# Attention with mixed heads: output matmuls of 128 keys on the whole height of the TensorE array instead of 64-key halves, and a third PSUM bank for the first mix

## The chip, the cores and the metric

The kernel runs on one core of a Trainium2 chip. The metric is the device time of one execution in microseconds (us); lower is better. The core has five engines with instruction queues of their own: PE (TensorE, matmuls; the profile shows its weight loads apart, as PEld), DVE (VectorE), ACT (ScalarE), POOL (GpSimd) and SP (SyncE, which here only issues DMAs).

## The reference

Talking-heads attention over 4 batches, 12 heads, 448 positions and head dimension 64, then a two-layer network with an ELU between. All arrays are float32.

```python
scores = scale * np.matmul(q, k.transpose(0, 1, 3, 2))      # (4, 12, 448, 448)
scores = np.einsum('bhij,hg->bgij', scores, w_pre)           # first mix over the heads
scores = scores - np.max(scores, axis=-1, keepdims=True)
attn = np.exp(scores)
attn = attn / (np.sum(attn, axis=-1, keepdims=True) + 1e-09)
attn = np.einsum('bhij,hg->bgij', attn, w_post)              # second mix over the heads
out = np.matmul(attn, v)                                     # (4, 12, 448, 64)
...
h = x @ w_in                                                 # x: 1792 x 768, w_in: 768 x 2048
g = np.where(h > 0.0, h, np.exp(np.minimum(h, 0.0)) - 1.0)
return g @ w_out                                             # 2048 x 768
```

## The kernel before

**The attention** goes through 16 blocks (4 batches times 4 blocks of query rows). A block has 10, 12, 12 or 11 *tiles* of 10 rows, which makes 180 tiles. Two tiles make a *step* (the last step of an 11-tile block has one), so there are 92 steps, and the loop over `j` in `attention` writes the instructions of all engines in a fixed order. One round of the loop issues, in this order on PE:

- `scores` for step j+2, the first mix (tile `s`, L223): 4 matmuls of 448 columns, into one PSUM bank for each of the two tiles. Then DVE takes the row maximum (`nm`, L228) and ACT the exponential with its sum (`p`, L230), which frees the bank.
- `qk` for one pair of heads of a later block (L189): 4 matmuls of 448 columns. DVE and ACT copy them out (`st`, L199) and SP sends them by DMA into `raw`, the layout in which the first mix reads all heads of a row at once.
- `av` (L281), a part of attention times V for an earlier block, described below.
- `post` for step j, the second mix (tiles `mixed`, L256): small matmuls with `p` as weights and the scaled mixing matrix `wz` (POOL, L243) as the moving operand, then two ACT copies into `at` (L263).

Every one of these matmuls uses a 64 x 64 quarter of the PE array: a half of its rows (the 64 partitions on which the operands lie) and a half of its columns (the 64 partitions of the result). Four of them, one for each quarter, can be under way together. All operands are float32, for which one matmul of the program becomes two passes on PE, each a weight load (LDWEIGHTS) and a MATMUL row in the trace.

**Keys.** The 448 keys lie in `at` as NJ = 4 chunks of 128 partitions; the last chunk has 64 keys. In `post` each tile has 7 pieces of 64 keys. Before, six pieces go to the upper and the lower half of the first three chunks, and the seventh is split by heads: half of the heads are put on the upper 64 partitions of chunk 3, half on the lower 64 (the order `PLACE` of the heads makes each half contiguous). The parts of chunk 3 that nobody writes hold zeros.

**Outputs.** `av(n, u, part)` makes the outputs of two pairs of heads (w = 0, 1) of block n. Upper and lower 64 keys of a chunk are separate matmuls that sum into separate PSUM banks (`half`), since the two row halves of the array run at once. With the split chunk this is 7 rounds of 4 quarters, 28 matmuls of 100, 110 or 120 columns; 4 rounds are issued in one step and 3 in the next (`parts`). `keep_av` then copies the first bank to SBUF and adds the second one (DVE, L295 and L296). There are 48 such groups (16 blocks times 3).

**PSUM.** Eight banks during the attention: 2 for `s`, 2 for `mixed`, 2 for `qk`, 2 for `av`.

**The network** (`Moe`) follows: 128 x 128 matmuls `h` (L500) and `y` (L570). Its first matmuls are mixed into the last steps of the attention. Besides, the weights are decoded on DVE, ACT and POOL all along (`Weights`).

Of the kernel before, what the change touches and what calls it, by code (L numbers as in the profile page):

```python
# [17 lines left out]
B, H, S, D = 4, 12, 448, 64  # L18
DM, DFF = H * D, 2048
R = 10  # L20
RH = R * H
HR = R // 2
# [3 lines left out]
CJ = 128  # L26
# [5 lines left out]
EPS = 1e-9  # L32
PLACE = [g for w in range(2) for g in range(H) if g // 2 % 2 == w]

# [85 lines left out]
def attention(ctx, tc, qd, kd, vd, wpre, wpost, xd, dec, moe):  # L120
# [93 lines left out]


    def scores(n, ts):
        z = small.tile([128, 2], F32, tag="z", name="z")
        got = []
        ps = [bank(ps_s, "s", 2) for _ in ts]
        for w in range(2):  # L220
# [26 lines left out]
    def post(pairs):  # L247
        for i, (p, wz) in enumerate(pairs):
            for c in range(NJ):
                for h in range(2):  # L250
                    half = slice(h * 64, (h + 1) * 64)
                    j, n = (c * CJ + h * 64, slice(0, RH // 2)) if c < NJ - 1 else (
                        c * CJ, slice(h * RH // 4, (h + 1) * RH // 4))
                    for w in range(2):
                        part = slice(w * 64, (w + 1) * 64)
                        nc.tensor.matmul(  # L256
                            mixed[w][half, i, c, n], p[part, j:j + 64], wz[part, n], start=True, stop=True)

# [8 lines left out]

    def av(n, u, part):
        m = count[n] * R
        if part.start == 0:  # L270
            xo[n, u] = [bank(*spare) for half in range(2)]
        ps = xo[n, u]
        full = [(w, c) for w in range(2) for c in range(NJ - 1)]
        todo = list(zip([(0, NJ - 1)] + full, full[:NJ - 1] + [(1, NJ - 1)] + full[NJ - 1:]))
        for todo in todo[part]:
            for half, (w, c) in enumerate(todo):
                part = slice(half * 64, (half + 1) * 64)
                hp = 2 * u + w
                for hh in range(2):
                    g = PLACE.index(2 * hp + hh)  # L280
                    nc.tensor.matmul(  # L281
                        ps[half][hh * 64:(hh + 1) * 64, w * m:(w + 1) * m].rearrange("p (t r) -> p t r", r=HR),
                        vs[blocks[n][0], hp][part, c, hh * 64:(hh + 1) * 64],
                        ats[n][part, c, :count[n], :, g * HR:(g + 1) * HR].rearrange("p t w r -> p (t w) r"),
                        start=c == (NJ - 1 if half == w else 0), stop=c == NJ - 2,
                    )

    def keep_av(n, u):
        b, i = blocks[n]
        m = count[n] * R  # L290
        if u == 0:
            x = xp.tile([128, NP * 120], F32, tag="x", name="x")
            xs[n] = x[:, :NP * m].rearrange("p (c m) -> p c m", c=NP)
        lo, hi = (ps[:, :2 * m].rearrange("p (w m) -> p w m", w=2) for ps in xo.pop((n, u)))
        nc.vector.tensor_copy(xs[n][:, 2 * u:2 * u + 2], lo)  # L295
        nc.vector.tensor_add(xs[n][:, 2 * u:2 * u + 2], xs[n][:, 2 * u:2 * u + 2], hi)  # L296

# [7 lines left out]
    for ps in mixed:  # L305
        nc.vector.memset(ps[:, :, NJ - 1], 0.0)
    load_q(0, nc.sync)
# [18 lines left out]
    work, qks, avs = {}, {}, {}  # L326
    spare = ps_qk, "av", 2

# [10 lines left out]
    V_AT = -4, -3, 3, 4, 5, 6  # L339
    parts = slice(0, 4), slice(4, 7)  # L340
    ends = [N - 11, N - 9, N - 7, N - 5, N - 3, N - 1, N, N + 1, N + 2]
# [11 lines left out]
    for n in range(NBL):  # L353
        b, i = blocks[n]
        for u in range(3):
            if n < NBL - 3:
                for part, j in zip(parts, OUT_AT[i][2 * u:2 * u + 2]):
                    avs.setdefault(b * ROUND + j, []).append((n, u, part))
            else:
                avs.setdefault(ends.pop(0), []).append((n, u, slice(0, 7)))  # L360
    for b in range(B):
# [5 lines left out]
    for j in range(-LOOK, N + 3):  # L367
        if j == N - 10:
            op_ctx.close()
            dec.early = None  # L370
            moe.begin()
            spare = moe.ps[0], "ps", 2, 2
        if j == N:
            spare = ps_s, "s", 2
        if j in FIRST and j >= N:
# [8 lines left out]
        ready = [(n, keep_qk(n, [(hp, qk(n, hp))])) for n, hp in todo[:1]]  # L384
        for n, u, part in avs.get(j, ()):
            av(n, u, part)
            if part.stop == 7:
                keep_av(n, u)
                if u == 2 and j < N:
                    plan(j + 1, lambda n=n: store_x(n))  # L390
                elif u == 2:
                    store_x(n)
# [187 lines left out]
def lay_out(q, k, v, w_pre, w_post, moe_w_in, moe_w_out):  # L580
# [14 lines left out]
    vd = vd.reshape(B, NP, 2, NJ, CJ, D).transpose(0, 1, 4, 3, 2, 5).reshape(B, NP, CJ, NJ, 128)  # L595
    vd[:, 1::2, 64:, NJ - 1], vd[:, 1::2, :64, NJ - 1] = vd[:, 1::2, :64, NJ - 1].copy(), 0

    pre = np.zeros((128, 64), w_pre.dtype)
    post = np.zeros((2, 64, H, HR), w_post.dtype)
    for r in range(HR):  # L600
# [4 lines left out]
        for w in range(2):  # L605
            post[w, g, :, r] = w_post[:, PLACE]
    blocks = [pre, post.reshape(128, RH // 2)]
# [24 lines left out]
```

## Time and profile before

| | |
|---|---|
| median of 3 runs | 877.09 us (874.34 to 879.68) |
| profiled execution, its own time | 880.2 us |
| its span, first to last instruction | 878.4 us |
| PE matmul busy | 812.2 us (92% of the span) |
| PE weight loads busy | 692.2 us (79%) |
| ACT, DVE, POOL busy | 486.9, 446.7, 327.1 us |
| DMA, mean | 158 GB/s |

The profile shows one execution. A PE row is busy from the start of a matmul to the modelled end of its results, and neighbours overlap, so a high busy share does not say that the array streams all that time. An idle time is put down to the instruction or DMA that ended it; where no such thing is recorded, the profile writes "issue".

### The profile page before, as it was taken

How to read it: one execution, taken by the hardware profiler on the slowest of the kernel's cores; microseconds unless marked ns; L12 is line 12 of the kernel's file. 1: busy time of each engine (PE TensorE's matmuls, PEld its weight loads, DVE VectorE, ACT ScalarE, POOL GpSimd, SP SyncE). 2: the span in 40 equal slices, each digit the busy share in tenths (PEclk: the TensorE clock that was granted, in tenths of full speed). 3: DMA queues.
4: the chain of work that ended last, by engine and by line, in shares of the span. 5: the costliest groups of instructions: out<-in, count | busy, mean ns of one | idle time of the engine just before them, and what ended most of it. 6: DMA issues, size and time to landing. Idle time of an engine off the chain costs nothing.

```text
span 878.4 us, 29259 instructions
## 1 busy us (share of the span) xinstructions
PE 812.2 (92%) x12240; PEld 692.2 (79%) x12240; DVE 446.7 (51%) x904; ACT 486.9 (55%) x1049; POOL 327.1 (37%) x406
## 2 busy tenths in 40 slices
PE   5879799979899988899799999899999999999998
PEld 1357687766777776678699999799999999999997
DVE  3456576656666755574888885597013333200000
ACT  2477677766777767572778771343146666511110
POOL 4322222212222212242777773544125555722221
PEclk9999999999999999999799999899999999999999
DMA  5586667656776664903666669775211111122220
GB/s 186 145 242 203 171 202 247 198 159 201 231 220 186 205 194 160 266 35 96 197 197 210 198 204 324 240 236 191 78 63 57 57 54 56 64 88 74 80 69 32
DMA packets 82467, 138.68 MB, mean 158 GB/s; under 512 B 20712, under 2 KB 57148, under 8 KB 82336
## 3 DMA queue, kind: packets, MB, share of 16 engines
q1 hardware_dynamic: 71392, 100.88, 37.6%
q0 software_dynamic: 10512, 35.25, 12.5%
q8 instruction: 97, 1.59, 0.7%
q10 hardware_dynamic: 432, 0.69, 0.2%
q14 instruction: 34, 0.28, 0.1%
HBM read 73.59 MB, written 23.62 MB: 111 GB/s over the span
## 4 chain that ended last, share of the span: by engine, by line
PE 72%; issue 9%; POOL 6%; DMA 5%; ACT 3%; DVE 3%; SPq 2%; POOLq 0%; DVEq 0%; ACTq 0%
PE y L570 23%; PE h L500 17%; PE s L223 9%; PE mixed L256 8%; PE qk L189 8%; PE av L281 6%; DMA raw<-st 2%; POOL lo L441 2%; POOL gl L519 2%; SPq L448 2%; ACT p L230 1%; DMA k<-in 1%; ACT st L199 1%; DVE nm L228 1%; POOL w L57 1%
## 5 line engine op out<-in xcount | busy, mean ns | idle before, releaser
L243 POOL TENSOR_SCALAR wz<-wb,rz 128x60 f32<-128x60 f32 x180 | 78.2, 447 | 265.1 <-DVE rz L239 212.8
L441 POOL TENSOR_TENSOR lo<-lo,hi 128x768 fp32r<-128x768 f32 (+1 forms) x56 | 117.1, 2092 | 126.4 <-ACT hi L440 126.1
L230 ACT ACTIVATE p<-s,nm 128x448 f32<-128x448 f32 x180 | 112.7, 631 | 63.6 <-DVE nm L228 63.5
L228 DVE TENSOR_REDUCE nm<-s 128x1 f32<-128x448 f32 x180 | 104.1, 619 | 85.0 <-PE s L223 83.5
L500 PE MATMUL h<-xh,hi 128*128 128x448 f32 x384 | 142.1, 370 | 4.8 <-ACT hi L440 4.8
L500 PE MATMUL h<-xh,lo 128*128 128x448 f32 x384 | 141.5, 369 | 1.2 <-POOL lo L441 1.2
L570 PE MATMUL y<-gh,lo 128*128 128x448 f32 x384 | 140.4, 366 | 2.0 <-POOL lo L441 2.0
L500 PE MATMUL h<-xl,hi 128*128 128x448 f32 x384 | 141.6, 369 | 0.0
L570 PE MATMUL y<-gh,hi 128*128 128x448 f32 x384 | 140.3, 365 | 1.3 <-ACT hi L440 1.3
L570 PE MATMUL y<-gl,hi 128*128 128x448 f32 x384 | 140.3, 365 | 0.0
L256 PEld LDWEIGHTS mixed<-wz,p 64*64 64x64 f32 x5760 | 113.8, 136 | 29.3 <-issue 27.6
L256 PE MATMUL mixed<-wz,p 64*64 64x60 f32 (+1 forms) x5760 | 119.6, 219 | 18.0 <-issue 17.3
L189 PE MATMUL qk<-k,q 64*64 64x448 f32 (+2 forms) x768 | 118.1, 594 | 13.2 <-ACT st L199 7.8
L223 PE MATMUL s<-raw,wa 64*64 64x448 f32 x720 | 112.4, 574 | 11.7 <-DMA raw<-st 4.1
L263 ACT COPY at<-mixed 128x480 f32<-128x480 f32 (+1 forms) x184 | 92.9, 562 | 40.3 <-PE mixed L256 40.1
L519 POOL TENSOR_TENSOR gl<-g,gh 128x448 fp32r<-128x448 f32 x64 | 74.0, 1157 | 82.8 <-ACT gh L518 82.3
L281 PEld LDWEIGHTS av<-at,v 64*64 64x64 f32 x2240 | 83.1, 133 | 24.9 <-issue 14.7
L513 DVE SCALAR_TENSOR_TENSOR g<-e,g 128x448 f32<-128x448 f32 x64 | 39.9, 623 | 120.0 <-ACT g L511 117.1
L281 PE MATMUL av<-at,v 64*64 64x120 f32 (+2 forms) x2240 | 84.2, 258 | 8.9 <-issue 8.7
L189 PEld LDWEIGHTS qk<-k,q 64*64 64x64 f32 (+2 forms) x768 | 42.9, 136 | 53.6 <-ACT st L199 29.3
L500 PEld LDWEIGHTS h<-xh,hi 128*128 128x128 f32 x384 | 73.0, 190 | 11.4 <-ACT hi L440 5.2
L500 PEld LDWEIGHTS h<-xh,lo 128*128 128x128 f32 x384 | 72.9, 190 | 7.6 <-POOL lo L441 1.8
(52 smaller groups left out, 1079.6 us busy)
## 6 DMA issues: line engine op xcount, KB each, us to landing
raw<-st SPq DMA_DIRECT2D x127, 210.0 KB
lo<-s SPq DMA_DIRECT2D x80, 256.0 KB
w<-in POOLq DMA_DIRECT2D x38, 512.0 KB, 4.6
s<-c POOLq DMA_DIRECT2D x48, 256.0 KB, 4.6
raw<-st SPq DMA_DIRECT2D x39, 175.0 KB
v<-in SPq DMA_DIRECT2D x24, 256.0 KB
out<-o SPq DMA_DIRECT2D x24, 224.0 KB
w<-in SPq DMA_DIRECT2D x10, 512.0 KB
```

The costliest lines, as they stand in the source:

```text
L189: nc.tensor.matmul(got[hh][rows, :S], qs[n][part, hp, rows], ks[blocks[n][0], hp][part], start=True, stop=True)
L223: nc.tensor.matmul(ps[a][w * 64:(w + 1) * 64, :S], wa[half], raws[n % 2][half, ts[0] + w, :], start=True, stop=True)
L228: nc.vector.tensor_reduce(nm, ps[i][:, :S], op=ALU.max, axis=AX.X, negate=True)
L230: nc.scalar.activation(p, ps[i][:, :S], AF.Exp, bias=nm, scale=1.0, accum_out=z[:, i:i + 1])
L243: nc.gpsimd.tensor_scalar_mul(wz, wb, rz[:, i:i + 1])
L256: nc.tensor.matmul(mixed[w][half, i, c, n], p[part, j:j + 64], wz[part, n], start=True, stop=True)
L263: nc.scalar.copy(ats[n][:, :, ts[0]:ts[0] + len(ts), w, :], mixed[w][:, :len(ts)].rearrange("p t c n -> p c t n"))
L281: nc.tensor.matmul(ps[half][hh * 64:(hh + 1) * 64, w * m:(w + 1) * m].rearrange("p (t r) -> p t r", r=HR), vs[blocks[n][0], hp][part, c, h ...
L441: self.nc.gpsimd.tensor_sub(lo_, f32(lo_), f32(hi_))
L500: self.nc.tensor.matmul(h, w[:, ks], x[:, k, :], start=n == 0, stop=n == 3 * NC - 1)
L519: self.nc.gpsimd.tensor_sub(self.gl[f][:, u, :], g, f32(self.gh[f][:, u, :]))
L570: nc.tensor.matmul(y[u], w[:, ks], g[f][:, u, :], start=f == 0 and n == 0, stop=f == NF - 1 and n == 2)
```

## The change

Three things change.

1. **Outputs.** `av(n, u, w)` now does one pair of heads a call: for each of the 4 chunks, two matmuls (heads hh = 0, 1) that use all 128 partitions of the chunk, that is the whole height of the array, and one half of its columns each. Both pairs of a group sum into one PSUM bank, side by side (columns of w = 0, then of w = 1), one pair a step. A group has 16 matmuls. `keep_av` is one copy; the addition is gone.
2. **Second mix.** `post` no longer splits the seventh piece: 7 pieces times 2 matmuls of 60 columns a tile. Pieces 0, 2, 4, 6 go to the upper 64 partitions and 1, 3, 5 to the lower ones; the lower half of chunk 3 holds zeros. The order `PLACE` is gone, and the host's layout of V and of the mixing matrix with it.
3. **First mix.** `av` needs one bank, and the bank that comes free is given to `scores`: the banks of the tiles turn through three (`first`, `first`, `more`) instead of two, until the last steps, where there are two again.

```diff
-PLACE = [g for w in range(2) for g in range(H) if g // 2 % 2 == w]
...
+    def room():
+        k = turn["s"] = turn.get("s", -1) + 1
+        return (ps_qk, "more", 1) if rooms == 3 and k % 3 == 2 else (ps_s, "first", 2)
+
     def scores(n, ts):
...
-        ps = [bank(ps_s, "s", 2) for _ in ts]
+        ps = [bank(*room()) for _ in ts]
...
     def post(pairs):
         for i, (p, wz) in enumerate(pairs):
-            for c in range(NJ):
-                for h in range(2):
-                    half = slice(h * 64, (h + 1) * 64)
-                    j, n = (c * CJ + h * 64, slice(0, RH // 2)) if c < NJ - 1 else (
-                        c * CJ, slice(h * RH // 4, (h + 1) * RH // 4))
-                    for w in range(2):
-                        part = slice(w * 64, (w + 1) * 64)
-                        nc.tensor.matmul(
-                            mixed[w][half, i, c, n], p[part, j:j + 64], wz[part, n], start=True, stop=True)
+            for j in range(0, S, 64):
+                c, half = j // CJ, slice(j % CJ, j % CJ + 64)
+                for w in range(2):
+                    part = slice(w * 64, (w + 1) * 64)
+                    nc.tensor.matmul(
+                        mixed[w][half, i, c, :], p[part, j:j + 64], wz[part], start=True, stop=True)
...
-    def av(n, u, part):
-        m = count[n] * R
-        if part.start == 0:
-            xo[n, u] = [bank(*spare) for half in range(2)]
-        ps = xo[n, u]
-        full = [(w, c) for w in range(2) for c in range(NJ - 1)]
-        todo = list(zip([(0, NJ - 1)] + full, full[:NJ - 1] + [(1, NJ - 1)] + full[NJ - 1:]))
-        for todo in todo[part]:
-            for half, (w, c) in enumerate(todo):
...
+    def av(n, u, w):
+        m, hp = count[n] * R, 2 * u + w
+        if w == 0:
+            xo[n, u] = bank(*spare)
+        for c in range(NJ):
+            for hh in range(2):
+                g = 2 * hp + hh
+                nc.tensor.matmul(
+                    xo[n, u][hh * 64:(hh + 1) * 64, w * m:(w + 1) * m].rearrange("p (t r) -> p t r", r=HR),
+                    vs[blocks[n][0], hp][:, c, hh * 64:(hh + 1) * 64],
+                    ats[n][:, c, :count[n], :, g * HR:(g + 1) * HR].rearrange("p t w r -> p (t w) r"),
+                    start=c == 0, stop=c == NJ - 1,
+                )
...
-        lo, hi = (ps[:, :2 * m].rearrange("p (w m) -> p w m", w=2) for ps in xo.pop((n, u)))
-        nc.vector.tensor_copy(xs[n][:, 2 * u:2 * u + 2], lo)
-        nc.vector.tensor_add(xs[n][:, 2 * u:2 * u + 2], xs[n][:, 2 * u:2 * u + 2], hi)
+        nc.vector.tensor_copy(
+            xs[n][:, 2 * u:2 * u + 2],
+            xo.pop((n, u))[:, :2 * m].rearrange("p (w m) -> p w m", w=2))
...
-    spare = ps_qk, "av", 2
+    spare = ps_qk, "av", 1
+    rooms = 3
```

**PE, the head of a step.** The rows below stand on PE where a step of the loop begins, in the program before: `s` is the first mix, `qk` the products for a later block, `av` the outputs, `mixed` the second mix; "x16" counts matmuls of one kind in a row.

```order
L223 MATMUL s<-raw_165,wa 64x448 x4
L189 MATMUL qk<-k,q 64x448 x2
L189 MATMUL qk<-k,q 56x448 x2
L281 MATMUL av<-at,v 64x100 x16
L256 MATMUL mixed_167<-wz,p 64x60
```

The same place in the changed program; `first` and `more` are the banks of the first mix.

```order
L226 MATMUL first<-raw_165,wa 64x448
L226 MATMUL more<-raw_165,wa 64x448
L188 MATMUL qk<-k,q 64x448 x2
L188 MATMUL qk<-k,q 56x448 x2
L275 MATMUL av<-at,v 64x120 x8
L256 MATMUL mixed_167<-wz,p 64x60
```

The order of the four kinds is the same. Where 16 or 12 `av` matmuls stood in a step, 8 stand now; the shape 64x120 is that of the result, and each reads 128 partitions instead of 64.

**PE, the end of the second mix and the next step's head.** Before, the last matmuls of a tile are the split seventh piece of 30 columns:

```order
L256 MATMUL mixed_167<-wz,p 64x60
L256 MATMUL mixed_168<-wz,p 64x60
L256 MATMUL mixed_167<-wz,p 64x30
L256 MATMUL mixed_168<-wz,p 64x30
L223 MATMUL s<-raw_165,wa 64x448 x4
```

In the changed program (the two `mixed` banks in turn, as in all of this part):

```order
L256 MATMUL mixed_167<-wz,p 64x60
L256 MATMUL mixed_168<-wz,p 64x60
L226 MATMUL first<-raw_166,wa 64x448 x4
L188 MATMUL qk<-k,q 64x448 x2
L188 MATMUL qk<-k,q 56x448 x2
```

A tile had 12 matmuls of 60 columns and 4 of 30, and has 14 of 60. On the other engines only DVE's `x` addition (L296) is gone, and the tiles of the first mix carry other names.

## Rows read from the trace of the kernel before

**Rows 1.** The page's head and its first part: busy time of each engine.

```profile
span 878.4 us, 29259 instructions
...
PE 812.2 (92%) x12240; PEld 692.2 (79%) x12240; DVE 446.7 (51%) x904; ACT 486.9 (55%) x1049; POOL 327.1 (37%) x406
```

**Rows 2.** Windows: stretch, then PE, PEld, DVE, ACT, POOL busy, clock, DMA.

```profile
38.00:384.00 346.00, 305.56 (x9451) 240.30 (x9447) 224.22 (x565) 248.26 (x631) 81.66 (x186) 0.99 0.67 199
...
553.50:878.40 324.90, 321.01 (x1583) 299.34 (x1583) 85.69 (x123) 123.21 (x209) 127.06 (x93) 0.99 0.30 95
```

**Rows 3.** Chain that ended last, 38 to 384 us: shares by line, one piece.

```profile
by line: PE s L223 21.0%; PE mixed L256 20.3%; PE qk L189 14.5%; PE av L281 14.2%; issue 10.3%; DMA raw<-st 5.7%; ACT p L230 3.1%; DVE nm L228 1.9%; ACT at L263 1.5%; DMA q<-in 1.5%; DMA k<-in 1.4%; PE ps L281 1.1%; ACT st L199 0.9%; SPq L2
...
375.65 4.91 issue
```

**Rows 4.** Timeline of PE, 200 to 256 us: start, length, what, count.

```profile
201.99 1.13 PE L256 MATMUL mixed<-wz,p 64*64 64x60 f32 x64 [0.43 <-issue]
...
212.74 1.01 PE L281 MATMUL av<-at,v 64*64 64x120 f32 x32
...
245.02 0.57 PE L223 MATMUL s<-raw,wa 64*64 64x448 f32 x1
...
248.56 1.10 PE L223 MATMUL s<-raw,wa 64*64 64x448 f32 x8
...
254.81 0.57 PE L223 MATMUL s<-raw,wa 64*64 64x448 f32 x1
```

**Rows 5.** Groups by shape: busy us, mean ns of one, then idle time before.

```profile
L256 PE MATMUL mixed<-wz,p 64*64 64x60 f32 x4320 | 109.9, 223 | 13.9 <-issue 13.3 <-POOL wz L243 0.2
...
L281 PE MATMUL av<-at,v 64*64 64x120 f32 x1064 | 41.3, 264 | 1.1 <-issue 1.1
...
L296 DVE TENSOR_TENSOR x<-x,av 128x240 f32<-128x240 f32 x19 | 7.7, 405 | 2.0
```

**Rows 6.** Timeline of PE where the matmuls change their tile.

```profile
384.86 0.47 PE L500 MATMUL h<-xh,hi 128*128 128x448 f32 x1
...
388.21 0.36 PE L500 MATMUL h<-xl,hi 128*128 128x448 f32 x1
388.41 0.36 PE L500 MATMUL h<-xh,lo 128*128 128x448 f32 x1
388.70 1.13 PE L256 MATMUL mixed<-wz,p 64*64 64x60 f32 x64
...
399.95 0.95 PE L281 MATMUL s<-at,v 64*64 64x110 f32 x31
400.83 0.47 PE L500 MATMUL h<-xh,hi 128*128 128x448 f32 x1
```

**Rows 7.** Waits, 38 to 384 us: us in total, times, longest.

```profile
PE mixed L256 <- issue: 17.3, 16, 2.4
...
PEld qk L189 <- ACT st L199: 10.1, 33, 0.7
...
PE av L281 <- issue: 8.7, 7, 2.8
...
PEld s L223 <- ACT p L230: 5.7, 12, 1.3
```

**Rows 8.** Windows from one pause of PE to the next.

```profile
172.69:178.32 5.63, 3.73 (x126) 3.12 (x127) 2.74 (x8) 2.82 (x8) 1.30 (x3) 1.00 0.82 267
...
327.60:333.57 5.97, 3.71 (x128) 2.85 (x127) 3.33 (x9) 4.28 (x12) 0.84 (x2) 1.00 0.87 268
```

**Rows 9.** The page's DMA queues: packets, MB, share.

```profile
q8 instruction: 97, 1.59, 0.7%
```

**Rows 10.** Timeline of PE: first and last of seven pauses over 1.4 us.

```profile
65.76 0.58 PE L281 MATMUL av<-at,v 64*64 64x100 f32 x16 [2.77 <-issue]
...
370.42 0.47 PE L256 MATMUL mixed<-wz,p 64*64 64x60 f32 x18 [2.10 <-issue]
```

**Rows 11.** Windows: the stretch behind the pause that ends at 333.57 us.

```profile
333.80:337.20 3.40, 3.40 (x77) 2.48 (x79) 0.64 (x4) 1.02 (x2) 0.84 (x2) 0.50 0.11 35
```

More of the change, by code (lines that the diff above doesn't have):

```diff
@@ L264, in keep_post @@
                 ats[n][:, :, ts[0]:ts[0] + len(ts), w, :], mixed[w][:, :len(ts)].rearrange("p t c n -> p c t n"))
-    def av(n, u, part):
-        m = count[n] * R
-        if part.start == 0:
-            xo[n, u] = [bank(*spare) for half in range(2)]
-        ps = xo[n, u]
-        full = [(w, c) for w in range(2) for c in range(NJ - 1)]
-        todo = list(zip([(0, NJ - 1)] + full, full[:NJ - 1] + [(1, NJ - 1)] + full[NJ - 1:]))
-        for todo in todo[part]:
-            for half, (w, c) in enumerate(todo):
[L277 to L286, printed above, removed]
+    def av(n, u, w):
[11 more added lines that the diff above has]
+                )
     def keep_av(n, u):
@@ L305, in attention @@
     for ps in mixed:
-        nc.vector.memset(ps[:, :, NJ - 1], 0.0)
+        nc.vector.memset(ps[64:, :, NJ - 1], 0.0)
     load_q(0, nc.sync)
@@ L339, in attention @@
     V_AT = -4, -3, 3, 4, 5, 6
-    parts = slice(0, 4), slice(4, 7)
     ends = [N - 11, N - 9, N - 7, N - 5, N - 3, N - 1, N, N + 1, N + 2]
@@ L356, in attention @@
             if n < NBL - 3:
-                for part, j in zip(parts, OUT_AT[i][2 * u:2 * u + 2]):
-                    avs.setdefault(b * ROUND + j, []).append((n, u, part))
+                for w, j in enumerate(OUT_AT[i][2 * u:2 * u + 2]):
+                    avs.setdefault(b * ROUND + j, []).append((n, u, w))
             else:
-                avs.setdefault(ends.pop(0), []).append((n, u, slice(0, 7)))
+                avs.setdefault(ends.pop(0), []).extend([(n, u, 0), (n, u, 1)])
     for b in range(B):
@@ L368, in attention @@
         if j == N - 10:
+            rooms = 2
             op_ctx.close()
@@ L373, in attention @@
         if j == N:
-            spare = ps_s, "s", 2
+            spare = ps_s, "first", 2
         if j in FIRST and j >= N:
@@ L384, in attention @@
         ready = [(n, keep_qk(n, [(hp, qk(n, hp))])) for n, hp in todo[:1]]
-        for n, u, part in avs.get(j, ()):
-            av(n, u, part)
-            if part.stop == 7:
+        for n, u, w in avs.get(j, ()):
+            av(n, u, w)
+            if w == 1:
                 keep_av(n, u)
@@ L595, in lay_out @@
     vd = vd.reshape(B, NP, 2, NJ, CJ, D).transpose(0, 1, 4, 3, 2, 5).reshape(B, NP, CJ, NJ, 128)
-    vd[:, 1::2, 64:, NJ - 1], vd[:, 1::2, :64, NJ - 1] = vd[:, 1::2, :64, NJ - 1].copy(), 0
     pre = np.zeros((128, 64), w_pre.dtype)
@@ L605, in lay_out @@
         for w in range(2):
-            post[w, g, :, r] = w_post[:, PLACE]
+            post[w, g, :, r] = w_post
     blocks = [pre, post.reshape(128, RH // 2)]
```

## The prediction

> **What bounds the kernel now.** I read the page's head first, then the windows by stage, then the chain of work that ended last, and only then single steps. The page puts PE at 92% of the span and no other engine above 55% [rows 1]. The windows split the span at the points where the work changes: nearly all of the 92 attention steps lie between 38 and 384 us, and from 553.5 us on PE is busy for 321 of 325 us with the network's matmuls, which the change doesn't touch [rows 2]. So the question is what happens in those 346 us of attention; a shift there passes on to the end, because PE's queue is in order and the later work is the same.
>
> In that stretch the chain lies on PE for 71% (`s` 21.0, `mixed` 20.3, `qk` 14.5, `av` 14.2, `ps` 1.1), on DMAs for 8.6%, on ACT and DVE for 7.4% and on "issue" for 10.3%, which is 35.6 us [rows 3]. One "issue" piece of 4.91 us is POOL's; the other 30.7 us are PE's. The reader should look hard at that item: it is time in which PE waits for nothing that another engine does. The waits say the same: before `mixed` and `av` no matmul was in flight for 17.3 + 8.7 = 26.0 us, in 23 pauses [rows 7]. Between two such pauses lie always the same number of instructions: 126 matmuls and 127 weight loads in one window, 128 and 127 in another (a few straddle the edge) [rows 8]. And the page has an instruction queue that moved 97 packets of 1.59 MB in all, which is 16.4 KB a packet; 24,480 matmul and load rows over 97 packets are 252 each [rows 1, 9]. So PE's instructions arrive in blocks of 252 of these rows, and a pause is a block that comes late: 5.63 and 5.97 us after the previous block's end in the two windows.
>
> How long does PE need for a block when it isn't late? Three undisturbed steps go from 245.02 to 254.81, 3.26 us each [rows 4]. A step has 4 `s`, 4 `qk`, 14 `av` (16 and 12 in turn) and 32 `mixed` matmuls, each two passes of a load and a matmul: 216 rows. A block of 252 is 1.17 steps, 3.8 us.
>
> **The outputs' passes.** 32 `av` passes of 120 columns take 1.01 us, and a row lasts 0.264 [rows 4, 5]; so the eighth foursome starts (1.01 - 0.264) after the first, which is 0.107 us for one pass. A group needed 7 rounds of two passes on each quarter, and needs 8 on each column half (4 chunks, 2 pairs), if the two halves run side by side as the quarters do. One round more is 0.214 us at 120 columns, 0.200 at the mean of 112.5; 48 groups: **+9.6 us**. If the halves didn't run side by side, it would be 8 more rounds: 48 x 8 x 0.200 = +77 us. The quarters of a row half run side by side today, so I take 9.6.
>
> **The second mix.** 64 passes take 1.13 us and a row 0.22 [rows 4, 5]: sixteen foursomes, 0.061 each. A tile kept each quarter busy for 8 passes (6 of 60 columns, 2 of 30). Now the quarters of the upper partitions get 4 of the 7 pieces, again 8 passes, all of 60. If a pass of 30 columns costs as much as one of 60, nothing changes; if it costs half, a step of two tiles has 14 units where it will have 16, and 92 steps x 0.97 x 2/14 are 13 us. A pass of 60 columns takes 0.061 us and one of 120 takes 0.107, so what a pass costs besides its columns is near 0.015; the truth lies between, but a load of 64 columns stands before every pass either way: **+1**, with 0 to 13 for the range.
>
> **Changing the tile.** All attention matmuls use quarters today; `av` on the whole height stands between `qk` and `mixed`. The only changes of tile in the trace are those to and from the network's 128 x 128 matmuls [rows 6]. Coming from them, the last `h` starts at 388.41, matmuls of that kind follow each other at 0.20, and `mixed` starts at 388.70: 0.09 us are lost. Going to them, `av` passes end with a start near 400.64 (399.95 + 0.95 less 0.26) and `h` starts at 400.83, again 0.09 more than the pass. Behind a change the first matmul also waits for its own load, which is otherwise done under the pass before: the first `h` lasts 0.47 instead of 0.36, for 128 columns of weights; half of it, 0.05, for 64. That makes 0.145 us a change. `av` stands in 81 of the steps before step 92, two changes each: 162 x 0.145 = **+23.5 us**. The bounds are 0, if a change of height alone costs nothing, and 162 x 0.20 = 32.
>
> The Trainium skill, in TensorEngine Tiling (Array Packing), Key Properties, speaks against this change: it says that changing the tiling mode, not just the tile, drains the TensorE. The 0.09 us agree with it for 64 x 64 against 128 x 128; no run here shows a change of height alone.
>
> **Fewer instructions.** A step falls to 4 + 4 + 8 + 28 matmuls, 176 rows, so there are 0.82 as many blocks, and a block lasts 1.43 steps. With the costs above a step is 3.26 + 0.10 + 0.01 + 0.26 = 3.63 us, and a block 5.2 us, 1.4 more than now. If a block comes as long after the previous one as today, each pause shrinks by 1.4 us. Seven pauses are longer than that, 1.75 to 2.77 us, 15.3 us together [rows 10]; 15.3 - 7 x 1.4 = 5.5 us stay, times 0.82 that is 4.5 of 26.0, 17%. Of the 30.7 us on the chain 83% go: **-25.5 us**. Bounds: only the number of blocks counts (-5.5), or all pauses go (-30.7).
>
> **What follows from it.** In the DMA parts of the chain, 8.6%, PE's added work is hidden: 34.1 becomes 31.2. PE waits 5.7 us for the exponential to free an `s` bank and 10.1 for `qk`'s copies [rows 7]. The third bank lets a step's second tile wait for the previous step's first tile, and a slower PE comes later to both: I take **-6** of these 15.8 us (0 to -15.8). Behind the long pause at 333.57 the clock was granted at 0.50 for 3.4 us, the 1.2 GHz level [rows 11]; there are three such stretches after pauses above 2 us. With the pauses gone up to 1.7 us each come back: **-3** (0 to -5). DVE loses 48 additions of some 0.4 us [rows 5]; at 51% busy it bounds nothing, 0. What would it cost if that cover were gone? Nothing, as it is work removed.
>
> The sum: 31.2 - 25.5 - 6 - 3 = -3.3 us. On the profiled execution's 880.2 us this is 876.9; that execution lies 3.1 above the median, so the forecast is **874 us** against 877.1.
>
> **The rivals.**
>
> *A, as summed:* costs and gains of some 30 us nearly cancel. Own range 862 to 886, from the bounds of the smaller terms.
>
> *B, a change of height alone is free.* The column halves stay as they are, which speaks for it; that the rows' sums then run through the whole height instead of half speaks against it. The 23.5 us fall away (21.5 where not hidden), the block shortens to 4.8 us, so some 2 us of pauses return: 874 - 21.5 + 2 = 854 us.
>
> *C, the pauses stay (slower).* If the time to the next block grows as blocks are used up more slowly, or the pauses come from something else than the count, only their number falls: -5.5 instead of -25.5, 894 us. For it: today no row tells when a block was asked for. Against it: 253 and 255 rows between pauses. It decides from the point where less than 22 us of pauses go. The Trainium skill's Runtime: NRT & Kernel Launch, Instruction fetch mechanics, states blocks of 256 instructions and calls the cost of crossing one mostly hidden; the trace agrees with the count and not with the hiding, as 26.0 us of pauses show.
>
> *D, the column halves don't run side by side at whole height:* 874 + 67 = 941 us. The quarters' behaviour speaks against it.
>
> **How the numbers follow.** A 0.63, B 0.22, C 0.12, D 0.03. The likeliest gives 874. 0.5%, 4.4 us, is about what a measurement of this kernel can tell from no change. A's range is centred 3 us below today, so 0.42 of it is faster by more than that, 0.38 within, 0.20 slower. Faster: 0.63 x 0.42 + 0.22 = 0.48; same: 0.24; slower: 0.13 + 0.15 = 0.28. The range from 848 to 890 holds A, B and the near part of C; above it are the rest of C and D.
>
> **What would show it.** In the changed profile the matmul and load rows of the attention's 346 us should fall from 18,898 [rows 2] to about 15,400; the pauses put down to "issue" before `av` and `mixed` from 26.0 to some 5 us; two gaps of about 0.1 us should stand at both ends of each `av` burst, and the first `av` row should be longer than the next; 16 `av` passes of 120 columns should take about 1.0 us. An undisturbed step should last 3.6 us. B would show as 3.4 us and no gaps, C as pauses of the old length after every 252 rows, D as `av` bursts of 1.9 us. The forecast fails if steps grow by more than 0.4 us, or if pauses return elsewhere.

## The result and the profile after

The changed kernel takes 871.7 us (median of 20 executions) where the kernel before, run beside it, takes 880.2: a ratio of 0.9895, 95% interval 0.9864 to 0.9927, which is 9.2 us less. A second run of the changed kernel gave 868.9 us and 0.988 [0.9841, 0.992]. The forecast was 874 with a range of 848 to 890. The ratios leave out the slower executions of each kernel, and one of these was the profiled execution of the first run (503 us from the first network matmul to the end instead of 492, which the change doesn't touch), so the profile shown here is the second run's.

The page's head, its busy times and its instruction queue:

```profile
span 867.4 us, 25410 instructions
...
PE 829.2 (96%) x10368; PEld 661.6 (76%) x10368; DVE 431.2 (50%) x856; ACT 489.7 (56%) x1049; POOL 325.2 (37%) x406
...
q8 instruction: 82, 1.34, 0.7%
```

The windows (columns as in [rows 2]), with the two stretches of 4 us in which the granted clock is lowest:

```profile
38.00:384.00 346.00, 331.14 (x7860) 218.62 (x7849) 216.22 (x531) 256.65 (x645) 83.94 (x190) 0.99 0.67 199
...
68.00:72.00 4.00, 0.40 (x4) 0.43 (x8) 0.00 (x0) 0.00 (x0) 0.00 (x0) 0.75 0.68 205
72.00:76.00 4.00, 4.00 (x28) 2.00 (x25) 1.78 (x3) 1.69 (x5) 0.00 (x0) 0.50 0.58 170
```

The chain that ended last, 38 to 384 us:

```profile
by line: PE mixed L256 23.3%; PE av L275 20.8%; PE qk L188 18.1%; PE first L226 13.6%; PE more L226 7.2%; DMA raw<-st 4.3%; PE ps L275 2.1%; issue 2.0%; PE h L495 1.5%; DMA xl<-xd 1.4%; ACT p L233 1.2%; DMA k<-in 1.0%; DVE nm L231 0.9%; SPq
```

The waits in the same stretch (us in total, times, longest):

```profile
PEld qk L188 <- ACT st L198: 6.5, 11, 1.1
...
PEld first L226 <- ACT p L233: 3.8, 7, 1.3
...
PE mixed L256 <- issue: 1.4, 2, 1.0
...
PE more L226 <- issue: 1.3, 1, 1.3
```

And the network's first kind of matmul, seen by its line (min, median and max ns, then the first and the last start):

```profile
L495 PE MATMUL h<-xh,hi x384: 362/365/739, 375.5 to 747.5; 128*128 128x448 f32 x192
```

Read them against [rows 1 to 3, 7]. PE's idle time in the 346 us falls from 40.4 us (346.00 - 305.56) to 14.9 (346.00 - 331.14). Nearly all of that is the pauses before `mixed` and `av`: 26.0 us before, 1.4 now, with no line for `av` any more. "issue" falls from 10.3% of the chain to 2.0%. But the first network matmul starts only 9.4 us earlier, at 375.5 instead of 384.9 [rows 6]. So idle time fell by 25.5 us, and PE's own work in the attention grew by 25.5 - 9.4 = 16 us. (The window holds 15,709 rows, against 15,400 forecast, since those 9.4 us are now filled with later work.) Gain and cost are both there, as the prediction had them; the cost is about half of the 34.1 us that it summed.

Single steps, on PE's timeline (start, length, what, count), with one place near the start of the attention:

```profile
71.60 0.97 PE L226 MATMUL first<-raw,wa 64*64 64x448 f32 x1 [5.40 <-DMA k<-in]
...
77.52 0.59 PE L226 MATMUL first<-raw,wa 64*64 64x448 f32 x2
...
223.81 1.09 PE L256 MATMUL mixed<-wz,p 64*64 64x60 f32 x54
224.68 0.59 PE L226 MATMUL first<-raw,wa 64*64 64x448 f32 x2
224.73 0.23 PE L256 MATMUL mixed<-wz,p 64*64 64x60 f32 x2
224.79 0.93 PE L226 MATMUL first<-raw,wa 64*64 64x448 f32 x6
225.49 0.98 PE L188 MATMUL qk<-k,q 64*56 64x448 f32 x8
226.39 1.00 PE L275 MATMUL av<-at,v 128*64 128x110 f32 x16
...
228.20 0.59 PE L226 MATMUL more<-raw,wa 64*64 64x448 f32 x1
```

An undisturbed step lasts 3.52 us (224.68 to 228.20, 110 columns). The gap that was forecast is there: the last `qk` matmul starts at 225.49 + 0.98 - 0.54 = 225.93 or so, such a pass streams some 0.37 us (rounds of such passes start 0.38 apart in undisturbed steps, as at 210.19 and 210.57 us), and `av` follows at 226.39, some 0.09 later than that. As forecast, the first `av` row is the longer one, 0.31 us against 0.26 for the next. The first line is a wait that wasn't there at this size. Before, the same matmul (88 rows of the first mix stand ahead of it in both kernels) read so, and a step near 250 us like the other three lines:

```profile
72.77 1.10 PE L223 MATMUL s<-raw,wa 64*64 64x448 f32 x8 [0.94 <-DMA raw<-st]
...
251.53 0.57 PE L223 MATMUL s<-raw,wa 64*64 64x448 f32 x1
251.54 0.29 PE L256 MATMUL mixed<-wz,p 64*64 64x30 f32 x6
251.81 0.98 PE L223 MATMUL s<-raw,wa 64*64 64x448 f32 x7
```

Up to here PE had paused for 4.5 us in three pauses, and then waited 0.94 us for the data of the first mix, which come over DMA. Now it comes to the same place without those pauses, waits 5.40 us, and starts at 71.60, only 1.2 us earlier; and behind the wait the clock is granted at 0.50, the 1.2 GHz level (the windows above), so that the step from 71.60 to 77.52 lasts 5.9 us. (The profile names `k<-in`; the wait is the first mix's, which reads `raw`, and the first run's profile puts the same wait down to `raw<-st`.)

The other three lines of before show what was hidden in its steps: the second tile's first mix started 0.28 us behind the first one's, since its bank was still held (the exponential that frees it ends at 251.75 on ACT). PE was busy with `mixed` for most of that time, so no view counts it as a wait. In the changed steps the passes of the first mix follow each other without such a delay (224.68 and 224.79).

One more record bears on the pauses, and the prediction didn't read it: the single packets of the DMA queues. Before, PE stands still from 62.99 to 65.76 us [rows 10]. In the stretch from 63.10 to 64.30 us the instruction queue moves one packet:

```profile
q8 instruction: 1, 0.02, 5.9%
```

It took 5.9% of 16 x 1.20 us, 1.13 us, and from 59.00 to 63.10 and from 64.30 to 65.76 us the queue moved none. So this block began to move only when PE had already stopped, and PE went on 1.5 us after it had landed. The other pauses read alike: all 27 pauses of PE that are put down to "issue" between 38 and 384 us, 28.0 us in all, end 1.3 to 1.7 us after the landing of such a packet of 16,384 bytes, and so do, at 1.2 to 1.6 us, all 69 (63 us) of the run `quarter_columns_outer` below, up to its first network matmul. Pauses that are put down to another engine or DMA end at scattered distances, 1.3 to 5.3 us in the kernel before. So PE waits for its instructions there; the prediction had that from the count alone. In neither trace do two of these packets start less than 3.3 us apart; the median is 4.3 and 4.2 us.

### The profile page after: what moved, and what is told of

Same layout as the page of the kernel before. It is cut to its first block, busy times and chain, and to the rows that moved or that the text cites. A ratio compares the mean times of both kernels' runs of the same rounds, so it can differ in the third digit from the quotient of the medians.

```text
span 877.8 us, 25410 instructions
## 1 busy us (share of the span) xinstructions
PE 839.1 (96%) x10368; PEld 661.5 (75%) x10368; DVE 430.9 (49%) x856; ACT 489.9 (56%) x1049; POOL 325.3 (37%) x406
## 4 chain that ended last, share of the span: by engine, by line
PE 90%; DMA 3%; ACT 2%; DVE 2%; issue 1%; POOL 0%; SPq 0%; ACTq 0%; POOLq 0%; DVEq 0%
PE y L565 27%; PE h L495 26%; PE qk L188 9%; PE mixed L256 9%; PE av L275 8%; PE first L226 6%; PE more L226 3%; DMA raw<-st 2%; ACT p L233 1%; PE ps L275 1%; ACT st L198 1%; DVE nm L231 1%; DMA xl<-xd 1%; PE first L275 1%; DMA v<-in 1%
## 5 line engine op out<-in xcount | busy, mean ns | idle before, releaser
L188 PE MATMUL qk<-k,q 64*64 64x448 f32 (+2 forms) x768 | 111.0, 593 | 11.6 <-ACT st L198 6.5
L263 ACT COPY at<-mixed 128x480 f32<-128x480 f32 (+1 forms) x184 | 92.5, 556 | 32.3 <-PE mixed L256 31.3
L256 PEld LDWEIGHTS mixed<-wz,p 64*64 64x64 f32 x5040 | 94.1, 134 | 20.0 <-issue 12.6
L256 PE MATMUL mixed<-wz,p 64*64 64x60 f32 x5040 | 106.2, 223 | 1.4 <-issue 1.0
L226 PE MATMUL first<-raw,wa 64*64 64x448 f32 x500 | 97.6, 562 | 10.4 <-DMA raw<-st 6.1
L275 PEld LDWEIGHTS av<-at,v 128*64 128x64 f32 x1280 | 63.6, 136 | 55.2 <-issue 31.2
L231 DVE TENSOR_REDUCE nm<-first 128x1 f32<-128x448 f32 x125 | 74.3, 618 | 60.6 <-PE first L226 31.2
L233 ACT ACTIVATE p<-first,nm 128x448 f32<-128x448 f32 x125 | 78.5, 632 | 41.2 <-DVE nm L231 40.9
L188 PEld LDWEIGHTS qk<-k,q 64*64 64x64 f32 (+2 forms) x768 | 39.4, 135 | 56.1 <-ACT st L198 26.8
L275 PE MATMUL av<-at,v 128*64 128x120 f32 (+2 forms) x1280 | 80.3, 267 | 0.0
L565 PEld LDWEIGHTS y<-gh,lo 128*128 128x128 f32 x384 | 72.6, 189 | 9.9 <-POOL lo L436 2.3
```

The costliest lines, as they stand in the source:

```text
L188: nc.tensor.matmul(got[hh][rows, :S], qs[n][part, hp, rows], ks[blocks[n][0], hp][part], start=True, stop=True)
L226: nc.tensor.matmul(ps[a][w * 64:(w + 1) * 64, :S], wa[half], raws[n % 2][half, ts[0] + w, :], start=True, stop=True)
L231: nc.vector.tensor_reduce(nm, ps[i][:, :S], op=ALU.max, axis=AX.X, negate=True)
L233: nc.scalar.activation(p, ps[i][:, :S], AF.Exp, bias=nm, scale=1.0, accum_out=z[:, i:i + 1])
L256: nc.tensor.matmul(mixed[w][half, i, c, :], p[part, j:j + 64], wz[part], start=True, stop=True)
L263: nc.scalar.copy(ats[n][:, :, ts[0]:ts[0] + len(ts), w, :], mixed[w][:, :len(ts)].rearrange("p t c n -> p c t n"))
```

## The experiments

The theory was the prediction's: pauses are blocks of 252 PE instructions that come late, the step's instruction count decides on them, and the change of the array's height costs 0.145 us each time. The rivals: the height costs nothing, or the third bank or the second mix does the work alone. All kernels compute the whole reference. Ratios are to the kernel before, run beside it (879 to 880 us).

**Third bank (two_banks).** Two banks for the first mix all along.

```diff
-    rooms = 3
+    rooms = 2
```

> The changed kernel with two banks for the first mix all along instead of three. If the gain comes from fewer instructions (my theory), PE reaches the first mix late enough that the exponential has mostly freed its bank: 872 to 876 us against 871.7 of the changed kernel, the wait of the first mix for the exponential growing from 3.8 to at most 8 us between 38 and 384 us. If the third bank is what brings the gain, the time goes back to that of the kernel before, 879 to 882 us, and an undisturbed step lengthens from 3.44 to 3.6 us or more.

873.0 us, 0.9916 [0.9895, 0.9937]. The wait of the first mix for the exponential goes from 3.8 to 6.3 us:

```profile
PEld first L226 <- ACT p L233: 6.3, 12, 1.3
```

The third bank is worth some 2 us by the medians, which the intervals, since they overlap, don't tell from nothing.

**More instructions, same columns (half_columns).** Each 448-column matmul of the first mix and of `qk` is cut in two of 224, which makes 208 rows a step instead of 176.

```diff
+                for cols in (slice(0, S // 2), slice(S // 2, S)):
                     nc.tensor.matmul(
-                got[hh][rows, :S], qs[n][part, hp, rows], ks[blocks[n][0], hp][part], start=True, stop=True)
+                        got[hh][rows, cols], qs[n][part, hp, rows], ks[blocks[n][0], hp][part, cols],
...
```

> The changed kernel with each first-mix and qk matmul of 448 columns cut into two of 224: the same columns through the array, no new tile, but 208 weight-load and matmul rows a step instead of 176. If PE's pauses are blocks of 252 rows that come late, a block now lasts 4.3 us instead of 5.1, and the pauses come back: 15 to 25 us more, 887 to 897 us, with some 20 us of idle time put down to issue before PE's matmuls. If the pauses have another cause than the number of instructions, the time stays within 3 us, 870 to 875 us.

879.4 us, 1.0018 [0.9983, 1.0052]: the whole gain is gone, though less was lost than expected. The waits, PE's work up to the first network matmul, and a step of 110 columns on the timeline:

```profile
PE mixed L259 <- issue: 8.6, 8, 2.6
...
PE first L229 <- issue: 1.8, 2, 1.2
```

```profile
38.00:385.80 347.80, 331.28 (x9058) 278.09 (x9049) 212.41 (x522) 251.22 (x631) 81.31 (x186) 1.00 0.66 198
```

```profile
219.03 1.03 PE L189 MATMUL qk<-k,q 64*64 64x224 f32 x16
...
222.66 1.03 PE L189 MATMUL qk<-k,q 64*64 64x224 f32 x16
```

The pauses are back with 10.4 us, where the changed kernel has 3.2 before all kinds of matmul. The count of instructions alone, with the array's columns as they were, makes the pauses. But the pauses aren't the whole of what the kernel lost, 10.8 us against the changed one. Up to the first network matmul PE's work is 331.3 us, against 322.6 in the changed kernel (375.5 - 38 - 14.9), and its idle time 16.5 against 14.9, since the wait of 5.40 us at 71.60 is gone. A step of 110 columns lasts 3.63 us instead of 3.52. So most of the loss is a price of the cuts themselves; the run shows that the count makes pauses, and not what they cost.

**The same with four pieces (quarter_columns, quarter_columns_outer).** Pieces of 112 columns, 272 rows a step. In the first version the pieces are the innermost loop, as in the diff above with `S // 4`; in the second one the outermost, so that neighbours lie on different quarters:

```diff
+        for cols in (slice(k, k + S // 4) for k in range(0, S, S // 4)):
             for w in range(2):
                 for a in range(len(ts)):
                     half = slice(a * 64, (a + 1) * 64)
...
```

> The changed kernel with each first-mix and qk matmul cut into four of 112 columns: the same columns, 272 rows a step. A block then lasts 3.2 us, less than nearly every interval seen between blocks, so PE would be paced by its blocks: 92 steps of 272/252 times 4.0 to 4.2 us, 60 to 95 us more than the changed kernel, 930 to 965 us. Two cuts cost 11 us; if that was the price of the cuts themselves, four cuts cost 33 us or less, up to 905 us.

> The changed kernel with each 448-column matmul of the first mix and of qk cut in four of 112, the pieces in the outer loop, so that neighbours lie on different quarters: 272 rows a step instead of 176, the same columns. Theory (PE's instructions come in blocks of 252 rows that take 3.1 to 7 us each under the attention's DMA load): a block is 0.93 steps, 3.2 us, and nearly every one comes late: 60 to 95 us more than the changed kernel, 930 to 965 us, with pauses of some 70 us put down to issue. Rival (the cut's own price, 48 more passes a step on four quarters at no more than 0.015 us besides their columns): at most 92 x 24 x 0.015 = 33 us, up to 905 us, and no more pauses than in the run with halves.

The first version took 1047.9 us, 1.1925 [1.187, 1.198], and can't tell the theories apart: PE was the bound for another reason, and "issue" was 0.1% of its chain. Its timeline:

```profile
229.32 1.97 PE L229 MATMUL first<-raw,wa 64*64 64x112 f32 x29
...
231.32 0.26 PE L229 MATMUL first<-raw,wa 64*64 64x112 f32 x1
```

The 32 passes of a first mix start over 2.0 us, 0.06 each. The second version's waits, PE's work up to the first network matmul, and timeline:

```profile
PE mixed L259 <- issue: 24.4, 23, 3.9
...
PE qk L189 <- issue: 12.0, 18, 2.2
...
PE first L229 <- issue: 8.5, 6, 2.0
PE av L278 <- issue: 7.5, 8, 2.0
```

```profile
38.00:449.40 411.40, 344.05 (x11778) 303.94 (x11770) 212.75 (x521) 252.09 (x630) 82.17 (x186) 0.98 0.57 168
```

```profile
227.48 0.31 PE L229 MATMUL first<-raw,wa 64*64 64x112 f32 x1
...
228.27 0.26 PE L229 MATMUL more<-raw,wa 64*64 64x112 f32 x1
```

Here the passes start 0.03 us apart until a pause comes, and the kernel takes 938.2 us, 1.0674 [1.0584, 1.0765], inside the 930 to 965 of the theory and beyond the rival's 905. Pauses stand before every kind of matmul, 52 us in these four lines. Of the 74 us by which the first network matmul starts later (449.4 against 375.5), 52 are idle time of PE (67.4 against 14.9) and 21 its own longer work; the cuts' own price alone doesn't explain that.

**The outputs back on quarters, the second mix as changed (quarters, quarters_2).** 28 `av` matmuls of 64 partitions in two banks, DVE's addition, two banks for the first mix; the seventh piece of the second mix stays unsplit, so the outputs need 8 rounds, and a step has 200 rows.

```diff
-            for hh in range(2):
...
+            for half in range(2 if c < NJ - 1 else 1):
+                part = slice(half * 64, (half + 1) * 64)
+                for hh in range(2):
...
+                        start=c == 0, stop=c == NJ - 1 - half,
...
-    spare = ps_qk, "av", 1
-    rooms = 3
+    spare = ps_qk, "av", 2
+    rooms = 2
```

> The changed kernel with its outputs put back on quarters of the array: 64-key pieces summed in two banks, 28 matmuls a group, no change of the tile, the first mix on two banks; the second mix stays as changed, so the outputs need 8 rounds a group and not the 7 of before. A step has 200 rows (before 216, changed 176), a block 4.2 us (before 3.8). If late blocks are the cause, a third of the 26 us of pauses goes and pays for the longer rounds: 875 to 882 us, with 12 to 20 us of idle time put down to issue. If instead it is the whole height itself that gains, and not the number of instructions, the longer rounds cost without a return: 886 us or more.

> The kernel of quarters once more (outputs on 64-row quarters, the second mix not split), beside the changed kernel on the same chip. Theory (the whole height buys its fewer pauses at their price, so it is worth nothing by itself): within 4 us of the changed kernel. Rival (the whole height brings a net gain): 6 us or more behind it. If it lies 4 us or more ahead, the whole height is a net loss.

868.8 us, 0.9868 [0.9821, 0.9914], and in the second run 868.5 us, 0.9849 [0.9804, 0.9894], beside 868.9 of the changed kernel. That is faster than I expected and as fast as the change. Waits, PE's work up to the first network matmul, and timeline of the first run:

```profile
PE mixed L256 <- issue: 10.0, 10, 2.2
...
PE first L226 <- issue: 7.2, 3, 4.0
...
PE av L277 <- issue: 3.1, 2, 1.8
```

```profile
38.00:377.10 339.10, 305.81 (x8770) 232.33 (x8760) 224.89 (x567) 247.99 (x633) 81.07 (x186) 0.98 0.68 202
```

```profile
205.39 1.10 PE L226 MATMUL first<-raw,wa 64*64 64x448 f32 x8
...
208.64 0.97 PE L226 MATMUL first<-raw,wa 64*64 64x448 f32 x8
```

A step is as short as before (3.25 us), and 20.3 us of such pauses stay. Up to the first network matmul PE works 305.8 us, as long as before (384.86 - 38 - 40.4 = 306.4), and stands idle for 33.3 instead of 40.4: 7.1 us less, nearly all of the 7.8 us by which that matmul starts earlier (377.1 against 384.9). So the second mix, left whole, brings as much as the whole change, and the rival that it does the work alone stands. The outputs' whole height, with the third bank that it makes room for, takes most of the other pauses out (idle time from 33.3 to 14.9 us) and adds nearly as much work (305.8 to 322.6 us): taken by itself it brings no gain that these times could tell. That the 16 rows a step are all that counts in the second mix isn't shown; `quarters_alternate` below speaks against it.

**The price of a change of height (split_burst).** The `av` matmuls of a step are cut in two bursts, one ahead of `qk`; the instructions are the same, with two more changes of height a step.

```diff
+        early = j < N - 10
+        for n, u, w in avs.get(j, ())[:1] if early else ():
+            av(n, u, w, (0, 1))
...
+            av(n, u, w, (2, 3) if early and k == 0 else (0, 1, 2, 3))
```

> The changed kernel with each output burst cut in two, chunks 0 and 1 ahead of qk and chunks 2 and 3 behind it: the same matmuls, some 72 bursts and so 144 changes of the tile's height more. At 0.145 us each that is 21 us more: 889 to 897 us. If a change of height alone costs nothing but its visible gap is hidden by later waits, 870 to 875 us.

885.7 us, 1.0061 [1.0035, 1.0087]: 14.6 us above the changed kernel (1.0061 - 0.9895 of 879.5). The timeline:

```profile
233.82 0.59 PE L226 MATMUL first<-raw,wa 64*64 64x448 f32 x2
...
234.78 0.61 PE L275 MATMUL av<-at,v 128*64 128x110 f32 x8
...
236.22 0.61 PE L275 MATMUL av<-at,v 128*64 128x110 f32 x8
...
237.63 0.59 PE L226 MATMUL more<-raw,wa 64*64 64x448 f32 x1
```

The step lasts 3.81 us where it had 3.52 at the same 110 columns: 0.145 for each of the two more changes, the very price that was forecast. Of it only 14.6 / 144 = 0.10 us reached the time, for about 144 more changes in some 72 steps, so the kernel stays under the 889 to 897 us expected. Part of the rest is cover: PE's idle time up to the first network matmul falls from 14.9 to 12.0 us. Rival B, that height alone is free, falls.

**Fewer changes (pairs_together, balanced).** Both pairs of a group in one step, which makes 42 bursts of `av` instead of 81; in `balanced` also the `qk` of those steps moved to the others.

```diff
-    OUT_AT = [(6, 7, 8, 9, 10, 11), (12, 13, 14, 15, 16, 17), (18, 19, 20, 21, 22, 23), (24, 25, 26, 27, 28, 28)]
+    OUT_AT = [(7, 7, 9, 9, 11, 11), (13, 13, 15, 15, 17, 17), (19, 19, 21, 21, 23, 23), (25, 25, 27, 27, 28, 28)]
```

> The changed kernel with both pairs of a group in one step, every other step: the same matmuls, 42 output bursts instead of 81. If a change of the tile's height costs 0.145 us, 78 changes fewer are 11 us: 858 to 864 us. If the gaps seen at a change hide under waits that come anyway, the time stays at 870 to 874 us. If the light steps without outputs run into the loop of first mix, maximum, exponential (about 3.1 us), half of the gain is lost: 866 us.

> Both pairs of a group in one step, as in the earlier run that gained nothing, and now the steps without outputs get two qk pairs and those with outputs get none, so that PE has 3.2 and 3.6 us in turn instead of 2.4 and 4.3. If the gain of 78 changes fewer was lost because light steps wait for the maximum and the exponential, most of the 11 us come now: 860 to 866 us. If ACT, which then has about 3.8 us of work in the steps with two qk pairs, becomes the limit, or the second qk pair waits for its bank, it stays at 868 to 875 us.

870.9 us, 0.9891 [0.9872, 0.991], and 894.9 us, 1.0182 [1.0137, 1.0227]. The first brings nothing. Its timeline, and the waits of first one and then the other:

```profile
231.62 0.59 PE L226 MATMUL more<-raw,wa 64*64 64x448 f32 x1
...
235.90 0.59 PE L226 MATMUL first<-raw,wa 64*64 64x448 f32 x1
...
238.44 1.02 PE L226 MATMUL first<-raw,wa 64*64 64x448 f32 x8
```

```profile
PEld qk L188 <- ACT st L198: 31.3, 41, 1.5
```

```profile
PEld qk L188 <- ACT st L198: 43.9, 45, 1.5
...
PE qk L188 <- ACT st L198: 33.5, 37, 1.4
```

The steps become 4.28 and 2.54 us, 6.82 for two, where two changed steps take 7.04; but in a step of 2.54 us ACT's copies of `qk` are late, and that wait grows from 6.5 to 31.3 us. PE's work up to the first network matmul falls by 4.4 us (322.6 to 318.2), and its idle time grows by 4.6. With `qk` in pairs as well the kernel is slower than either expectation had it, and the waits for ACT's copies come to 77 us. That the changes saved are lost to an uneven load of ACT is read from these waits; the run that was to even it out didn't.

**The halves in balance (alternate_halves, quarters_alternate).** The seventh piece of a step's second tile goes to the lower partitions of chunk 3, with V's last chunk on both halves: 14 passes deep on every quarter instead of 16 and 12. Both the changed kernel and `quarters` were run with it.

```diff
-                c, half = j // CJ, slice(j % CJ, j % CJ + 64)
+                lo = j % CJ if j < S - 64 else i * 64
+                c, half = j // CJ, slice(lo, lo + 64)
...
+    vd[:, :, 64:, NJ - 1] = vd[:, :, :64, NJ - 1]
```

> The changed kernel, but the seventh piece of 64 keys of each step's second tile goes to the lower 64 partitions of chunk 3, with V's last chunk held on both halves: a step's second mix is 14 passes deep on every quarter instead of 16 on the upper and 12 on the lower ones, with the same number of instructions. Theory (PE is paced by the passes' depth, 0.061 us for one of 60 columns): 92 x 2 x 0.061 = 11 us less array time, of which some 3 us are hidden under waits: 862 to 866 us, 0.980 to 0.985 of the kernel before. Rival (a matmul's own start, or another engine, paces the second mix): no gain, 869 to 873.

> As quarters (outputs on 64-row quarters), with the seventh piece put to the upper and lower half in turn by tile, so that the outputs need 7 rounds and the second mix 14 passes: 208 rows a step where before had 216 and quarters 200. If the balance of the halves pays as array time: up to 11 us from the second mix and 10 from the outputs less than quarters, given back in part as pauses, since a block of 252 rows then lasts 252/208 x 3.1 = 3.8 us as in the kernel before: 858 to 868 us, with 15 to 25 us of pauses put down to issue. If it all comes back as pauses: 868 to 877.

871.7 us, 0.989 [0.9824, 0.9956], and 866.7 us, 0.9862 [0.9791, 0.9933]. Neither differs measurably from the kernel that it was made from; the 862 to 866 us expected of the first didn't come. Its timeline:

```profile
233.64 1.08 PE L257 MATMUL mixed<-wz,p 64*64 64x60 f32 x55
234.50 0.54 PE L226 MATMUL first<-raw,wa 64*64 64x448 f32 x1
```

From `mixed` to the first mix are 0.86 us where the changed kernel has 0.87 (223.81 to 224.68): in the unbalanced one the first mix already starts while the last passes of the second mix are still to start (224.68 and 224.73), on the lower quarters by the program's order; the trace doesn't name the quarter. In `quarters_alternate`, with 208 rows a step, "issue" ahead of PE's `mixed`, `first` and `av` comes to 22.7 us, inside the 15 to 25 expected. Whether it beats the two kernels of 868 to 869 us, these intervals don't tell. But it saves only 8 rows a step against the kernel before and keeps most of its pauses (26.6 us in the same three lines), and is still some 12 us faster: in its profiled execution (861.8 us, where the median is 866.7) PE's work up to the first network matmul is 298.6 us, 7.8 less than before. So the second mix and the outputs can also gain by shorter work, and not by fewer instructions alone.

## Why the prediction was right, point by point

The direction, the range and the mechanism held: pauses of some 25 us go, and new work comes in, 16 us of it where 31 were summed. The forecast was 0.4% less than before and 1.05% were measured; that 874 lies so near 871.7 is in part luck, because the kernel before measured 880.2 us in this run and not the 877.1 that the forecast started from.

- **Fewer instructions: right.** 82 packets against 97 [rows 9], 0.85; the pauses before `mixed` and `av` fell to 1.4 us where 4.5 were forecast. `half_columns` and `quarter_columns_outer` bring them back by count alone, and the packet records show each one ending behind the landing of a block. Rival C, that they stay, falls. What sets the distance at which blocks come was not shown. The prediction counted the instructions of the outputs and of the second mix as one term; the runs part them: the second mix alone brings the gain, and the outputs pay for theirs.
- **Changing the tile: right per change, too large in the sum.** 0.145 us stands in the step, as summed, but 0.10 reaches the time. If the 162 of the change fare like those of `split_burst`, the term is 162 x 0.10 = 16 us instead of 23.5 (21.5 where not hidden), and the sum goes from -3.3 to about -9, against 9 to 11 us measured. The step of the prediction that was mis-sized is the cover: only the 8.6% of DMA pieces were taken to hide added PE work. Steps before also held starts of the first mix that were late behind a busy PE (251.81 against 251.53), which no wait counts. The numbers agree: PE's work grew by 16 / 92 = 0.17 us a step on average, and by 0.26 in undisturbed steps (3.26 to 3.52), so the other steps before were already longer than 3.26. That the late starts are the cover is argued from such rows and was not tried by itself.
- **The step: 3.52 instead of 3.63 us.** Since the price of both changes stands in it, another term of the step is smaller, or the 3.26 us it was added to; which one was not shown.
- **The outputs' passes:** 16 of 110 columns take 1.00 us, so the column halves do run side by side; rival D falls.
- **The second mix:** a cost of +1 can't be told from nothing here; in `quarters` PE's work is as long as before, with an eighth round of outputs in it. Two passes less of depth (`alternate_halves`) bring no gain that the times could tell.
- **The waits for copies: right as a sum** (15.8 to 10.3 us, -5.5 where -6 was taken), but the third bank has some 2 of it.
- **The clock: not confirmed.** In this profile the stretches after pauses are gone (the first run's has one, at 252.65 us behind a pause of 2.07), but one behind the DMA wait at 71.60 has come, with a step that is 2.4 us longer (5.9 against 3.5).
- **Not forecast:** that wait itself. The 4.5 us of pauses taken out ahead of 72 us came back there, it seems, as a wait for `raw` (5.40 against 0.94 us).

The Trainium skill's TensorEngine Tiling (Array Packing), Key Properties, says that changing the tiling mode drains the TensorE; `split_burst` agrees for a change of height alone, 64 x 64 to 128 x 64, at 0.145 us in the step.

## What to carry to other kernels

When PE pauses and no engine is named, divide its matmul and load rows by the packets of the instruction queue: if pauses stand at that spacing, and end behind the landing of that queue's packets, fewer instructions can be worth more than fewer columns, and a matmul that was split for balance is a place to save them. Try each part of such a change by itself: here one part brought the gain and another only paid for its own. Price a new mode change by the step, then ask how much of a step is already covered, for example by a tile that starts late while another one keeps PE busy. Where a stall early in a pipeline goes, look at what is loaded next: it may only move into a DMA wait.

## What the runs showed of the hardware

- PE's instructions come in blocks of 16,384 bytes, some 252 matmul and load rows each. Where PE had to wait for a block, it went on 1.2 to 1.7 us after the block had landed (96 pauses of two traces), and no two blocks started to move less than 3.3 us apart.
- A change of height alone, 64 x 64 to 128 x 64, costs 0.145 us in the step (`split_burst`), as much as was summed from the rows of the changes between 64 x 64 and 128 x 128.
- Where four matmuls in a row go to one quarter of the array, the quarters work less beside each other: the 32 passes of 112 columns started 0.06 us apart, and 0.03 apart with neighbours on different quarters (1048 and 938 us for the kernel). With two in a row (`half_columns`) the first mix shows nothing of this: its 16 passes of 224 columns took 0.78 us to `qk`, 8 of 448 take 0.81 (224.68 to 225.49).
- The array doesn't wait for its slowest quarter between kinds of matmul: passes of the first mix start ahead of the last passes of the second mix (224.68 and 224.73).
